# A hand-ordered attention and mixture-of-experts kernel: the written order of all engines replaced by another, and the first zero matmuls cut into more pieces

## The chip, the cores and the metric

The kernel runs on one core of a Trainium2 chip. A core has five engines with a queue of instructions each: TensorE (PE; its weight loads are shown as PEld), VectorE (DVE), ScalarE (ACT), GpSimd (POOL) and SyncE (SP), which here only issues transfers. The metric is the device time of one execution in microseconds (us); lower is better.

## The reference, cut to what matters

Two stages over 8 batches of 576 positions. The first is attention with a window of 64 keys, for 8 heads of 64; the second takes its result as input of four causal attention experts, of which each position uses two.

```python
scores = scale * np.matmul(q, k.transpose(0, 1, 3, 2))
scores = np.where((rel >= 0) & (rel < 64), scores, -1e9)
x = softmax(scores) @ v                      # heads side by side: 8 x 576 x 512
logits = x @ w_gate                          # the two largest of four, softmax over the two
for e in range(4):
    a = softmax(causal(scale * (x @ wq[e]) @ (x @ wk[e]).T))
    out += gate[e] * (a @ (x @ wv[e]) @ wo[e])
```

## The kernel before

The work is cut into units, and a unit into steps: a generator yields after each step. The string `ORDER` names a unit at each word, and each word runs the next step of that unit. Since every step only appends instructions to the queues of the engines it uses, `ORDER` alone sets in which order the work stands on all five engines. Digits behind a colon are the PSUM banks that the step takes.

The units that matter below, with their lines in the profile:

- `f`: first constants. DVE zeroes the tile `px`, and TensorE runs matmuls of zeros on it (L214). `c` and `i` are other constants (`causal`, `m_f`, `tri`).
- `m`: scores of the first stage (L337). One word computes two groups, which are 64 matmul instructions of 96 columns on a quarter of the array's columns and half of its rows, each with its own weight load. Two such words after each other are 128 matmuls and 128 loads.
- `q`: softmax of a group (DVE L349 to L386, ACT L365, POOL L362, L384, L390). `t`: its transposes (L407). `a`: product with the values (L433).
- `w`: weights split into two half-precision parts (L266 is their TensorE step). `n`, `M`, `N`: one scale per batch (L483 and L488 on TensorE, L491 on DVE).
- `v`, `k`, `r`, `o`: projections to values, keys, queries and output, all on L585 to L587, three matmuls for each product. `x` and `y`: scores and softmax of the second stage (L701, L710; DVE L721, ACT L725). `u`: its gates and splitting (ACT L772, POOL L782 and L783). `D`: transposes of the weights by a transfer, the last three on TensorE (L800). `A`: product with the values (L832, then ACT L838 and DVE L841).
- `F`: matmuls that compute nothing that is used (L874), in `keep_busy`; the number behind the underscore says how many.
- `p`, `h`, `l`: loads of queries and keys, of values, and of weights, issued by SP.

TensorE's instructions come from DRAM through a queue of their own, which the profile calls "q8 instruction".

Of the kernel before, what the change touches and what calls it, by code (L numbers as in the profile page):

```python
# [38 lines left out]


ORDER = (
# [104 lines left out]
def window_attention_moe_attention(ctx: ExitStack, tc: tile.TileContext, qT, kT, vW,  # L146
                                   wg, wq, wk, wv, wo, out):
    nc = tc.nc
# [8 lines left out]
    def bank():  # L157
        return PS[:, banks.pop(0)]
# [46 lines left out]
    def first_constants():  # L205
# [7 lines left out]
        for _ in range(8):  # L213
            nc.tensor.matmul(bank(), lhsT=px[:, 0:128], rhs=px[:, None].to_broadcast([128, 2, 256]),  # L214
                             start=True, stop=True)
# [298 lines left out]
    M2 = {}  # L514
# [475 lines left out]
```

## Time and profile before

| what | value |
|---|---|
| three runs | 414.85, 413.15, 412.34 us; median 413.15 |
| profiled execution, its own time | 414.9 us |
| its span, first to last instruction | 413.1 us |
| TensorE busy | 384.6 us, 93% of the span |
| DVE, ACT, POOL busy | 342.1, 333.3, 301.3 us |
| mean granted TensorE clock | 0.981 |
| "q8 instruction" | 56 transfers, 0.92 MB |

The span is the time from the first instruction to the last, and 1.8 us of the execution lie outside it. Busy times overlap between engines. A granted clock of 1.00 is 2.4 GHz, 0.50 is 1.2 GHz; a value between them is a stretch with some of both. In a row of waits, "A <- B" means that A stood still until B ended; "issue" stands where an engine waited for nothing that the profile shows.

### The profile page before, as it was taken

To read this page: it belongs to the slowest core of one execution; us is meant where nothing else is said; L and a number is where in the kernel's file an instruction comes from. 1 tells how busy PE (TensorE), PEld (TensorE's weight loads), DVE (VectorE), ACT (ScalarE), POOL (GpSimd) and SP (SyncE) were. 2 spreads that over 40 slices of the span, in tenths; PEclk is the share of its full clock that TensorE was granted. 3 is DMA by queue.
4 is the path that set the end of the run, shared out by engine and by line. 5 is a ranking of instruction groups with operands and counts; after the bars stand their busy time and mean duration, and the time that the engine had idled before them with its cause. 6 is when DMAs were issued, how large, how long until landed. Compare 5 with 4: busy or idle time off the path is not lost. (4 is left out here: it accounts for less than half of the span.)

```text
span 413.1 us, 18175 instructions
## 1 busy us (share of the span) xinstructions
PE 384.6 (93%) x7234; PEld 285.7 (69%) x7234; DVE 342.1 (83%) x1044; ACT 333.3 (81%) x1150; POOL 301.3 (73%) x678
## 2 busy tenths in 40 slices
PE   6879997899899998999999999999999999999884
PEld 3757874778577874777677776678677876876553
DVE  2969999987898876888999988798898898699841
ACT  1949599986999975898898899877899789879851
POOL 7346757989889986788878988688888976976300
PEclk9989999999999998999999999999999999999968
DMA  7951621699979977785984999896889852799973
GB/s 238 376 172 66 209 81 69 136 200 163 219 240 176 206 137 171 180 230 89 146 260 108 222 177 254 256 168 130 151 189 219 131 85 85 126 201 187 187 124 111
DMA packets 141732, 71.04 MB, mean 172 GB/s; under 512 B 122576, under 2 KB 125648, under 8 KB 141648
## 3 DMA queue, kind: packets, MB, share of 16 engines
q1 hardware_dynamic: 141280, 69.50, 78.2%
q8 instruction: 56, 0.92, 0.9%
q10 hardware_dynamic: 368, 0.39, 0.3%
q14 instruction: 28, 0.23, 0.2%
HBM read 30.94 MB, written 9.44 MB: 98 GB/s over the span
## 5 line engine op out<-in xcount | busy, mean ns | idle before, releaser
L783 POOL TENSOR_TENSOR sp<-p,sp 128x320 f16<-128x320 f32 (+3 forms) x110 | 100.0, 909 | 9.2
L725 ACT ACTIVATE p<-p,r 128x576 f32<-128x576 f32 (+3 forms) x128 | 77.4, 609 | 6.5 <-DVE r L721 6.4
L772 ACT ACTIVATE sp<-p,r 128x576 f16<-128x576 f32 (+3 forms) x122 | 72.7, 620 | 2.2 <-DVE r L761 0.9
L365 ACT ACTIVATE p<-ps,st 128x64 f32<-128x64 f32 x204 | 61.3, 315 | 11.6 <-POOL st L362 11.3
L721 DVE CUSTOM_DVE_ANT_0 p<-ps,causal,sc 128x320 f32<-128x320 f32 (+2 forms) x128 | 64.2, 546 | 6.2 <-PE ps L710 5.2
L782 POOL TENSOR_SCALAR p<-p,r 128x320 f32<-128x320 f32 (+3 forms) x110 | 65.4, 594 | 4.5 <-ACT sp L772 3.5
L390 POOL TENSOR_TENSOR p<-p,st 128x256 f32<-128x256 f32 x72 | 43.5, 614 | 12.7 <-DVE st L386 10.4
L411 DVE TENSOR_TENSOR pt<-ps,tri 128x1024 f32<-128x1024 f32 (+1 forms) x40 | 44.0, 1104 | 1.9 <-PE ps L407 1.9
L433 PE MATMUL ps<-pt,vt 64*64 64x128 f32 (+1 forms) x1440 | 39.2, 249 | 4.7 <-DVE r L721 1.7
L365 ACT ACTIVATION_READ_ACCUMULATOR p<-ps,st 128x1 f32 x204 | 42.5, 208 | 0.0
L710 PE MATMUL ps<-kt,qt 64*128 64x320 f16 (+3 forms) x480 | 40.4, 292 | 1.6 <-DVE pt L411 0.9
L433 PEld LDWEIGHTS ps<-pt,vt 64*64 64x64 f32 x1440 | 34.3, 133 | 11.1 <-DVE r L721 3.4
L337 PE MATMUL ps<-k,q 64*32 64x96 f32 (+2 forms) x2304 | 36.6, 245 | 5.4 <-issue 4.4
L832 PE MATMUL ps<-tu,v 128*64 128x64 f16 (+2 forms) x1056 | 39.6, 231 | 0.9 <-DMA tu<-sp 0.9
L832 PEld LDWEIGHTS <-v 128*64 128x64 f16 x1056 | 36.0, 113 | 5.5 <-issue 3.3
L337 PEld LDWEIGHTS ps<-k,q 64*32 64x32 f32 x2304 | 29.5, 106 | 12.1 <-issue 7.3
L585 PE MATMUL ps<-wvhi,xh 128*128 128x260 f16 x128 | 35.8, 279 | 1.8 <-DVE xl L460 1.4
L585 PE MATMUL ps<-xh,wqhi 128*128 128x320 f16 (+1 forms) x128 | 36.8, 287 | 0.4 <-DVE p L372 0.3
L585 PE MATMUL ps<-xh,wkhi 128*128 128x256 f16 (+1 forms) x128 | 36.7, 286 | 0.3 <-DVE v L611 0.3
L586 PE MATMUL ps<-xl,wkhi 128*128 128x256 f16 (+1 forms) x128 | 36.6, 286 | 0.0
L587 PE MATMUL ps<-xh,wklo 128*128 128x256 f16 (+1 forms) x128 | 36.6, 286 | 0.0
L587 PE MATMUL ps<-xh,wqlo 128*128 128x320 f16 (+1 forms) x128 | 36.6, 286 | 0.0
(165 smaller groups left out, 1016.0 us busy)
## 6 DMA issues: line engine op xcount, KB each, us to landing
vt<-in_vW_dram SPq DMA_DIRECT2D x16, 576.0 KB, 6.1
q<-in_qT_dram SPq DMA_DIRECT2D x14, 576.0 KB, 5.3
k<-in_kT_dram SPq DMA_DIRECT2D x14, 576.0 KB, 6.4
out_dram<-out SPq DMA_DIRECT2D x30, 256.0 KB, 2.9
tu<-sp SPq DMA_TRANSPOSE x93, 4.1
out_dram<-out SPq DMA_DIRECT2D x9, 128.0 KB, 3.0
q<-in_qT_dram SPq DMA_DIRECT2D x2, 320.0 KB, 8.3
k<-in_kT_dram SPq DMA_DIRECT2D x2, 320.0 KB, 7.7
```

What stands on the lines that cost most here:

```text
L337: nc.tensor.matmul(S1[g][o:o + 32, i, c:c + n], lhsT=q_t[r, i % 2, q0:q0 + 32], rhs=k_t[r, i % 2, k0:k0 + n], start=True, stop=True)
L365: nc.scalar.activation(pt[:, i], ps[:, i, 64:128], AF.Exp, bias=st[:, 0, z + i:z + i + 1], scale=0.125, accum_out=st[:, 1, z + i:z + i + 1])
L411: nc.vector.tensor_tensor(t, src, tri[:, None].to_broadcast([128, 2 * n, 2, 64]), op=OP.mult)
L433: nc.tensor.matmul(to, lhsT=values[d][r, h, b + e - (w == 0)], rhs=rhs, start=(e, h) not in started, stop=s == n - 1, skip_group_check=True)
L585: nc.tensor.matmul(ps, lhsT=ah, rhs=bh, start=first, stop=False)
L587: nc.tensor.matmul(ps, lhsT=al, rhs=bh, start=False, stop=last)
L721: nc.vector.tensor_tensor_reduce(out=dst, in0=src, in1=mask, scale=SC[b][:, 3:4], scalar=above, op0=OP.add, op1=OP.min, accum_out=to)
L725: nc.scalar.activation(p, p, AF.Exp, bias=r2[:, 0, x:x + 1], scale=-1.0, accum_out=r2[:, 1, x:x + 1])
L772: nc.scalar.activation(hi, p, AF.Copy, scale=by)
L782: nc.gpsimd.tensor_scalar(p, p, by, 1.0, op0=OP.mult, op1=OP.mult)
L783: nc.gpsimd.tensor_tensor(lo, p, hi, op=OP.subtract)
L832: nc.tensor.matmul(to, lhsT=V2[b % 2][:, c, a, 2 * pr + h], rhs=rhs, start=n == 0, stop=n == len(work_list) - 1, skip_group_check=True)
```

## The change

The string `ORDER` is replaced as a whole. All units and all steps are the same, each as often as before; their order and their banks differ. The `F` words differ too: five with 31 matmuls before, ten with 38 now, and the first three of them use `px` in place of `ident`. The eight matmuls of zeros of 512 columns in `f` become 53 of 73 to 86 columns, with the same columns in sum: a bank takes seven or six of them, by the digits of `FILL`.

```diff
+FILL = "77777666"
 
 ORDER = (
-    'p0 i c p1 h0 l0 f:01234567 l2 h1 p0 z p1 l1 m0:6 l3 d q0 h2 q0 e1 m1:7 q0 e0 q0 m2:5 q1 q0 m3:0 q1 n0 q1 q1 q1 '
...
+    'f:01234567 p0 c p1 l0 l2 h0 h1 z i p0 Fa0_3:0 m2:7 p1 m0:6 d l1 l3 q0 e0 q2 Fa1_4:5 m3:5 q0 q0 q0 m1:4 e1 w0 q1 '
...
 )
@@ first_constants
-        for _ in range(8):
-            nc.tensor.matmul(bank(), lhsT=px[:, 0:128], rhs=px[:, None].to_broadcast([128, 2, 256]),
-                             start=True, stop=True)
+        for n in map(int, FILL):
+            ps = bank()
+            for i in range(n):
+                c = slice(512 * i // n, 512 * (i + 1) // n)
+                nc.tensor.matmul(ps[:, c], lhsT=px[:, 0:128], rhs=px[:, 0:c.stop - c.start], start=True, stop=True)
```

The lines of the changed program are higher by four: L337 is L341 there, and so on. Three places show what the new order does. The first is the start of DVE's queue, before the first scores. Before:

```order
L225 MEMSET tri 128x128
L551 MEMSET m_f 128x128
L558 TENSOR_SCALAR causal<-m_f 64x64
L559 TENSOR_SCALAR causal<-m_f 64x64
L560 TENSOR_SCALAR m_f<-m_f 128x64
L206 MEMSET px_72 128x128
L207 MEMSET half_87 128x2
L208 MEMSET win 128x64
```

The same place on DVE in the changed program:

```order
L208 MEMSET px_72 128x128
L209 MEMSET half_87 128x2
L210 MEMSET win 128x64
L555 MEMSET m_f 128x128
L562 TENSOR_SCALAR causal<-m_f 64x64
L563 TENSOR_SCALAR causal<-m_f 64x64
L564 TENSOR_SCALAR m_f<-m_f 128x64
L229 MEMSET tri 128x128
```

Zeroing `px`, on which TensorE's first matmuls wait, moved ahead of all other constants.

The second place is on TensorE, between a product `a` of the fourth batch and the output projection of an earlier one. Before:

```order
L433 MATMUL ps<-pt_30_2836,vt_84 64x64 x4
L433 MATMUL ps<-pt_30_2836,vt_84 64x128 x12
L433 MATMUL ps<-pt_30_2836,vt_84 64x64 x4
L337 MATMUL ps<-k_2498,q_2497 32x96 x32
L407 MATMUL ps<-ident,p_33_2859 128x64 x4
L407 MATMUL ps<-ident,p_34_2902 128x64 x4
```

On TensorE in the changed program, the same product and what stands behind it; a row of L341 or L437 is two matmuls and two loads for each of its count, one of L411 is one of each:

```order
L437 MATMUL ps<-pt_30_2971,vt_84 64x64 x4
L437 MATMUL ps<-pt_30_2971,vt_84 64x128 x12
L437 MATMUL ps<-pt_30_2971,vt_84 64x64 x4
L411 MATMUL ps<-ident,p_33_2969 128x64 x4
L411 MATMUL ps<-ident,p_34_3006 128x64 x4
L589 LDWEIGHTS y_109
L589 MATMUL ps<-wohi,y_109 128x512
```

On TensorE in the changed program, a little further on, at the end of the first product of the projection:

```order
L590 LDWEIGHTS y_110
L590 MATMUL ps<-wolo,y_110 128x512
L591 LDWEIGHTS y_110
L591 MATMUL ps<-wohi,y_110 128x512
L341 MATMUL ps<-k_2611,q_2610 32x96 x32
L589 LDWEIGHTS y_109
L589 MATMUL ps<-wohi,y_109 128x512
```

The word of `m` with its 64 score matmuls moved from ahead of the transposes to behind six matmuls of 512 columns.

The third place is on TensorE in the second batch of the first stage. Before:

```order
L407 MATMUL ps<-ident,p_18_1242 128x64 x4
L407 MATMUL ps<-ident,p_19_1366 128x64 x4
L337 MATMUL ps<-k_1190,q_1189 32x96 x32
L433 MATMUL ps<-pt_16_1471,vt_84 64x64 x4
L433 MATMUL ps<-pt_16_1471,vt_84 64x128 x12
L433 MATMUL ps<-pt_16_1471,vt_84 64x64 x4
L433 MATMUL ps<-pt_17_1548,vt_84 64x64 x4
```

The same units on TensorE in the changed program:

```order
L437 MATMUL ps<-pt_16_1514,vt_84 64x64 x4
L437 MATMUL ps<-pt_16_1514,vt_84 64x128 x12
L437 MATMUL ps<-pt_16_1514,vt_84 64x64 x4
L341 MATMUL ps<-k_1244,q_1243 32x96 x32
L411 MATMUL ps<-ident,p_18_1293 128x64 x4
L411 MATMUL ps<-ident,p_19_1420 128x64 x4
L437 MATMUL ps<-pt_17_1595,vt_84 64x64 x4
```

The product of group 16 moved ahead of the scores and of the transposes.

## Rows read from the trace of the kernel before

**Rows 1.** The page, busy time, share of the span and instructions of each engine.

```profile
PE 384.6 (93%) x7234; PEld 285.7 (69%) x7234; DVE 342.1 (83%) x1044; ACT 333.3 (81%) x1150; POOL 301.3 (73%) x678
```

**Rows 2.** Windows: stretch, length, busy time (instructions) by engine, TensorE clock, DMA share, GB/s.

```profile
20.00:30.00 10.00, 6.90 (x127) 5.04 (x110) 5.92 (x17) 4.74 (x19) 4.82 (x7) 0.83 0.48 152
150.00:200.00 50.00, 47.66 (x894) 34.39 (x891) 41.15 (x127) 38.04 (x133) 38.60 (x91) 0.97 0.74 160
200.00:250.00 50.00, 49.15 (x913) 35.78 (x913) 46.53 (x145) 45.44 (x165) 41.93 (x90) 1.00 0.95 190
390.00:400.00 10.00, 7.49 (x87) 5.27 (x82) 5.96 (x19) 6.38 (x14) 0.76 (x1) 0.69 0.98 165
```

**Rows 3.** Waits of TensorE: us in total, times, longest.

```profile
PE ps L337 <- issue: 4.4, 2, 2.4
...
PE ps L433 <- DVE r L721: 1.7, 2, 1.4
```

**Rows 4.** Timeline of TensorE around three stops: start, length, instructions, idle before.

```profile
18.97 1.68 PE L337 MATMUL ps<-k,q 64*32 64x96 f32 x123
23.07 0.36 PE L337 MATMUL ps<-k,q 64*32 64x96 f32 x5 [2.42 <-issue]
...
160.38 0.36 PE L337 MATMUL ps<-k,q 64*32 64x96 f32 x6 [1.96 <-issue]
...
268.43 0.27 PE L433 MATMUL ps<-pt,vt 64*64 64x64 f32 x2 [0.68 <-issue]
```

**Rows 5.** Windows from one stop to another, the third in part of the second.

```profile
23.05:160.36 137.31, 128.15 (x2678) 98.15 (x2678) 119.70 (x350) 114.73 (x433) 105.92 (x236) 0.99 0.73 166
160.36:268.42 108.06, 105.84 (x2042) 76.42 (x2042) 95.39 (x290) 92.82 (x324) 87.05 (x188) 0.98 0.88 187
255.25:268.42 13.17, 12.30 (x255) 7.99 (x256) 10.41 (x30) 12.14 (x39) 9.90 (x20) 1.00 1.00 271
```

**Rows 6.** The page, DMA queue of TensorE's instructions: packets, MB, share.

```profile
q8 instruction: 56, 0.92, 0.9%
```

**Rows 7.** DMA queues from 13.8 to 20.6 us, all that moved.

```profile
q1 hardware_dynamic: 1434, 2.55, 97.2%
q14 instruction: 1, 0.01, 0.4%
```

**Rows 8.** DMA queues from 157 to 158 us.

```profile
q8 instruction: 1, 0.02, 5.8%
```

**Rows 9.** Windows of short stretches without a stop.

```profile
305.89:309.27 3.38, 3.38 (x127) 2.65 (x130) 3.38 (x10) 2.86 (x6) 3.13 (x7) 1.00 1.15 104
115.10:118.35 3.25, 3.25 (x138) 3.02 (x131) 3.16 (x8) 3.25 (x9) 2.09 (x6) 1.00 0.63 190
```

**Rows 10.** Windows in which the clock was at half.

```profile
25.10:28.50 3.40, 2.75 (x13) 1.92 (x13) 2.66 (x5) 3.12 (x17) 0.97 (x3) 0.50 0.84 271
161.64:165.05 3.41, 3.41 (x10) 1.18 (x8) 3.10 (x7) 0.00 (x0) 1.44 (x4) 0.50 1.02 75
393.75:400.57 6.82, 6.35 (x57) 4.19 (x56) 3.35 (x9) 2.78 (x7) 0.00 (x0) 0.50 0.83 125
```

**Rows 11.** Waits of the other engines from 155 to 170 us.

```profile
ACT out L861 <- PE ps L587: 4.4, 1, 4.4
...
DVE ps L352 <- PE ps L337: 2.6, 1, 2.6
```

**Rows 12.** Timeline of TensorE, groups of small matmuls.

```profile
154.94 1.53 PE L832 MATMUL ps<-tu,v 128*64 128x256 f16 x36
156.40 1.12 PE L433 MATMUL ps<-pt,vt 64*64 64x64 f32 x40
157.47 0.95 PE L337 MATMUL ps<-k,q 64*32 64x96 f32 x58
```

**Rows 13.** Timeline of TensorE, matmuls that keep it busy, and transposes at half clock.

```profile
3.98 3.59 PE L214 MATMUL ps<-px 128*128 128x512 f16 x8 [3.98 <-DVE half L207]
...
9.78 2.72 PE L874 MATMUL ps<-ident 128*128 128x128 f32 x22
...
394.04 1.78 PE L800 MATMUL ps<-ident_h,sp 128*128 128x128 f16 x15 [0.21 <-ACT sp L772]
```

199 rows, old and new, of the table ORDER are left out of this document.

## The prediction

> **What bounds the kernel now.** I read the busy times first. TensorE is busy for 384.6 us of 413.1, the others for 301 to 342 [rows 1], so where TensorE stands still is the first question. Windows by stage answer it: from 200 to 250 us it is busy for 49.15 of 50 us at full clock, but it loses 3.1 us of the ten from 20 to 30, 2.3 us from 150 to 200, and 2.5 us of the ten from 390 to 400, and in the same three windows the mean clock is 0.83, 0.97 and 0.69 [rows 2]. The list of waits then shows that the largest item is none of an engine's: "issue", 4.4 us in two pieces ahead of the score matmuls [rows 3]. The timeline puts them at 20.65 to 23.07 and at 158.42 to 160.38, each in the midst of an unbroken run of equal matmuls, with a third one of 0.68 us at 268.43 [rows 4]. Nothing in the program waits there: 123 matmuls of a word go through, and the last five wait for 2.42 us.
>
> What they have in common is their place in TensorE's own stream. Between the first and the second stop it ran 2678 matmuls and 2678 weight loads, 5356, which is 20 short of 21 times 256; between the second and the third 4084, 12 short of 16 times 256; and the stretch from 255.25 to 268.42 has 511, one short of two times 256 [rows 5]. The instructions that are missing are those that only wait, which the view doesn't count. The queue that brings TensorE's instructions made 56 transfers of 0.92 MB, 16 KB each [rows 6], and 14468 matmuls and loads divided by 56 are 258. So the stops are ends of a block of 256 instructions whose successor had not arrived. The Trainium skill, "Runtime: NRT & Kernel Launch", section "Instruction fetch mechanics", gives the same block (16 KiB, 256 instructions) and says that the next one is fetched while the current one executes, so that crossing a boundary is "mostly hidden". The trace agrees with the size [rows 5, 6] and disagrees with the second at these three ends, with 2.42, 1.96 and 0.68 us [rows 4]; by that rule the change would be worth nothing, which is a rival below.
>
> Why these ends and not the other fifty: from 13.8 to 20.6 us not one block came, while loads held 97.2% of the DMA engines [rows 7]; the block before the second stop came between 157 and 158 us [rows 8], and TensorE went on at 160.38. So from its start a block needs 2.4 to 3.4 us until it can be used, and its start is late where loads fill the queues. A block of instructions that TensorE finishes faster than that makes it stand. Stretches of about 256 that took 3.38 and 3.25 us show no stop [rows 9], so the limit without loads in the way is below 3.3 us.
>
> **The change part by part.**
>
> *The blocks.* I cut TensorE's order of both programs into blocks of 256 and priced their small matmuls by the timeline: a score matmul with its load 0.016 us (58 in 0.95; 0.014 in the long run of 123), a product of the first stage 0.028 (40 in 1.12), one of the second stage 0.0425 (36 in 1.53) [rows 4, 12]. Before, the block that ends at the first stop holds 124 score matmuls, 1.7 us of work; the one that ends at the second 59 scores, 40 and 29 products, 3.3 us; the one at the third 86 and 30 products and 12 wide matmuls, over 3.7 us, which was late for loads alone. In the changed order the poorest block is the third place shown: 64 scores and 52 products, 2.5 us, with eight transposes and three wide matmuls on top. The next hold 32 and 36 products with 45 scores (3.2 us and 15 others), and 34 scores with 84 products (3.0 us and ten others). The burst of 128 scores near 20 us is still there, but the pieces of `f` and the added `F` words push the block's end into its middle: 69 scores end a block that begins some 30 matmuls and 12 busy-keeping ones earlier. At the second place six wide matmuls now stand between the products and the scores. So the first stop, 2.42 us, and the second, 1.96, should go; the third, 0.68, too if the loads stand as before, since its block is mixed otherwise.
>
> What is late next there: nothing with a claim on the same time. In the second stop DVE waited 2.6 us for those scores, and ACT 4.4 us for the projection behind them [rows 11]; in the window of the first DVE is busy for 5.92 of 10 us and ACT for 4.74 [rows 2]. All engines come forward with TensorE.
>
> *The clock.* Behind the first two stops the granted clock falls to 0.50, 1.2 GHz, from 25.10 to 28.50 and from 161.64 to 165.05 [rows 10]; before that TensorE had stood for 2.42 and 1.96 us. At full clock the busy time in them is half: 2.75/2 is 1.4 us and 3.41/2 is 1.7 us less. I take 3.1; bounds 0 (the clock falls for another reason) and 3.4.
>
> *New stops.* The poorest block costs nothing if its successor starts at once (limit below 3.3 us), and up to 3.4 less 2.5, 0.9 us, if not; late by a load as in rows 7, some 2.4 us, and then the clock's 1.7 too. I take 0.5 for it and 0.5 each for the next two, in sum 1.5; bounds 0 and 6.
>
> *Zero matmuls.* They start when DVE has zeroed `px`, at 3.98 us before, and that memset is now DVE's first [rows 13]. The eight took 3.59 us. 53 pieces of the same columns take as long if the columns bound them. If a load of 128 columns bounds each, the nearest row is the transposes of 128 columns at half clock, 1.78 us for 15, 0.12 each, and 53 are 6.3 us. Either ends at 4.5 to 7.5 us after a start near 1 us, and the scores began at 7.5. I take 0, as weights and values that are still loading bound that stage; bounds -1 and 0.
>
> *More `F` matmuls.* One costs 2.72/22, 0.12 us for each of two records, so seven more cost 1.7 us [rows 13]. Most stand in the first 30 us, where TensorE waits; two words with five matmuls stand later, 1.2 us. I take 0.3; bounds 0 and 1.2.
>
> *All else* of the order: no term can be read off a table of words; bounds -2 and +3, taken as 0. The last 20 us keep their shape (transposes by TensorE between waits for splits, half clock for 6.82 us [rows 10]), with one output projection put behind the last product.
>
> The sum: -2.42 - 1.96 - 0.68 - 3.1 + 1.5 + 0.3 is -6.4 us. From the profiled execution's 414.9 this makes 408.5. Its time is 1.75 above the median of the three, 413.15, so the forecast is 406.8 us.
>
> **The rivals.**
>
> *The stops move.* Lateness follows the loads, and the new order has its own coincidences: loads of queries, keys and values stand next to the blocks with 45 and 34 scores. Two stops of 2.2 us, each with 1.6 us of clock, are 7.6 instead of 1.5; 406.8 + 6.1 is 412.9, no change. For it: the third stop befell a block that wasn't short. Against: two of the three went with the two poorest blocks.
>
> *The stops aren't the instructions.* Then another order has them somewhere else or they cost nothing once others bound the stage: 413.2 give or take 1. Rows 5 speak against it. This is what the skill's "mostly hidden" would give.
>
> *Slower.* The order pays for its long blocks with overlap: score words that stand behind six wide matmuls reach DVE later, and TensorE then waits for probabilities at L433 as it does once now, for 1.4 us [rows 3]. It decides once this happens oftener than (6.4 + 4.1)/1.4, about eight times, once in each batch: 417.3 us and more. Against it: from 200 to 250 us DVE and ACT still have 3.5 and 4.6 us of 50 free [rows 2].
>
> *The change doesn't do what it says.* A block as short as 1.7 us is gone by count, so this is only open for the poorest one, and is in its term.
>
> **How the numbers follow.** A measurement of this kernel tells about 1% from no change, 4.1 us. The forecast, with both long stops gone and the rest within its bounds, 402 to 409 us: 0.62. Stops that move, 409 to 413.5: 0.22; of it 0.02 is still faster. Not the instructions: 0.06. Slower within 1%: 0.02. Slower by more: 0.08. So faster 0.64, same 0.28, slower 0.08. The low end of the range is 406.8 less the 1.5 of new stops, 1 of the start and 2 of the rest, about 402; the high end is the second case's, 413.5. Outside lie the slower cases, 0.10, half of the 0.06, and some 0.05 of the forecast's own below 402.
>
> **What would show it.** Right: no wait of the kind "issue" over 1 us in a run of equal matmuls, a clock of 1.00 from 10 to 390 us, the matmuls of the first batch's scale (L492 there) without a stop ahead of them, and no half clock near 160 us. Wrong: a stop of 2 us at another multiple of 256, most likely in a block with 45 or 34 scores; or none, with TensorE's waits for DVE and ACT between 50 and 350 us grown by more than 4 us.

## The result, and the profile after

| | before | changed |
|---|---|---|
| median, runs beside each other (6 and 6) | 412.59 us | 408.58 us |
| again, beside the experiments (14 and 6) | 412.57 us | 408.38 us |
| profiled execution, and its span | 414.9, 413.1 us | 407.6, 405.9 us |

The ratio is 0.989, 95% interval 0.986 to 0.992, and 0.988 (0.984 to 0.992) in the second comparison: the change makes the kernel faster, by 4.0 and 4.2 us. Medians here and below are of the runs that are within 1.5% of the fastest of the same kernel. The two profiled executions lie further apart than that, 7.2 us of span, since that of before was the slowest of its first three runs and that of the changed kernel the fastest of its six. The programs of the experiments are longer or shorter by a few lines too, so that L337 of before is L338 in one and L341 in another.

The page of the changed kernel, its busy times and the queue of TensorE's instructions [rows 1, 6]:

```profile
PE 384.2 (95%) x7293; PEld 288.3 (71%) x7293; DVE 347.7 (86%) x1044; ACT 333.3 (82%) x1150; POOL 302.1 (74%) x678
...
q8 instruction: 57, 0.93, 1.0%
```

TensorE is as long busy as before, in a span that is 7 us shorter. That is not the same work at the same speed: 12.5 us of the busy time of before lie in windows at half clock [rows 10], and this profile of the changed kernel has none; its `F` words, on the other hand, are busy for 11.7 us where they were for 8.0. The same stages as in rows 2:

```profile
20.00:30.00 10.00, 9.24 (x197) 7.14 (x197) 8.96 (x24) 6.81 (x25) 6.69 (x12) 1.00 0.61 217
150.00:200.00 50.00, 48.48 (x894) 34.42 (x895) 44.23 (x137) 41.39 (x142) 42.05 (x95) 1.00 0.91 206
200.00:250.00 50.00, 49.76 (x1069) 37.97 (x1060) 44.65 (x143) 46.30 (x168) 42.16 (x96) 1.00 0.86 170
390.00:400.00 10.00, 9.45 (x128) 6.93 (x126) 4.92 (x14) 5.79 (x14) 0.00 (x0) 1.00 0.55 158
```

The stage of the first stop gained 2.3 us of work in ten, and the clock is 1.00 in all four. The head of the list of waits of TensorE [rows 3]:

```profile
PE ps L437 <- DVE r L725: 2.1, 2, 1.5
PE ps L836 <- DMA tu<-sp: 1.9, 1, 1.9
PE ps L487 <- DVE st L390: 1.4, 1, 1.4
...
PE ps L590 <- DVE xl L464: 1.0, 1, 1.0
...
PE ps L589 <- DVE v L615: 0.8, 1, 0.8
PE ps L705 <- DVE kt L680: 0.8, 1, 0.8
```

"issue", 4.4 us before, is no longer among the large items; waits for other engines and for a transfer stand there, among them two that rows 3 did not have at this size (L487 in the start, L836 in the tail). The timeline of the changed kernel at the place of the second stop, and at the only end of a block that still shows one [rows 4]:

```profile
159.89 1.12 PE L341 MATMUL ps<-k,q 64*32 64x96 f32 x64
160.95 1.01 PE L437 MATMUL ps<-pt,vt 64*64 64x64 f32 x40
...
259.40 0.57 PE L836 MATMUL ps<-tu,v 128*64 128x64 f16 x17 [0.27 <-issue]
```

The 64 score matmuls run through, and the only stop left is 0.27 us by this view.

### The profile page after: what moved, and what is told of

Same layout as the page of the kernel before. It is cut to its first block, busy times and chain, and to the rows that moved or that the text cites. A ratio compares the mean times of both kernels' runs of the same rounds, so it can differ in the third digit from the quotient of the medians.

```text
span 405.9 us, 18314 instructions
## 1 busy us (share of the span) xinstructions
PE 384.2 (95%) x7293; PEld 288.3 (71%) x7293; DVE 347.7 (86%) x1044; ACT 333.3 (82%) x1150; POOL 302.1 (74%) x678
## 4 chain that ended last, share of the span: by engine, by line
PE 63%; DVE 18%; ACT 7%; POOL 5%; issue 4%; DMA 0%; ACTq 0%; POOLq 0%; DVEq 0%
PE ps L589 13%; PE ps L590 12%; PE ps L591 12%; PE ps L714 7%; PE ps L836 6%; PE ps L341 5%; PE ps L437 5%; DVE p L725 4%; PE ps L411 2%; DVE pt L415 2%; ACT p L369 2%; DVE sp L780 2%; ACT p L729 1%; DVE ps L356 1%; ACT xh L462 1%
## 5 line engine op out<-in xcount | busy, mean ns | idle before, releaser
L776 ACT ACTIVATE sp<-p,r 128x448 f16<-128x448 f32 (+3 forms) x122 | 73.3, 619 | 2.4 <-DVE r L765 1.4
L437 PE MATMUL ps<-pt,vt 64*64 64x128 f32 (+1 forms) x1440 | 38.9, 249 | 3.6 <-DVE r L725 2.1
L836 PE MATMUL ps<-tu,v 128*64 128x64 f16 (+2 forms) x1056 | 39.4, 229 | 2.6 <-DMA tu<-sp 1.9
L437 PEld LDWEIGHTS ps<-pt,vt 64*64 64x64 f32 x1440 | 33.9, 133 | 10.5 <-DVE r L725 3.5
L836 PEld LDWEIGHTS <-v 128*64 128x64 f16 x1056 | 35.6, 111 | 7.9 <-issue 4.7
L341 PE MATMUL ps<-k,q 64*32 64x96 f32 (+2 forms) x2304 | 38.3, 245 | 0.3 <-DVE xl L464 0.3
L590 PE MATMUL ps<-xl,wqhi 128*128 128x320 f16 (+1 forms) x128 | 36.6, 286 | 1.0 <-DVE xl L464 1.0
L589 PE MATMUL ps<-xh,wqhi 128*128 128x320 f16 (+1 forms) x128 | 36.7, 287 | 0.9 <-DVE v L615 0.8
L589 PE MATMUL ps<-xh,wkhi 128*128 128x320 f16 (+1 forms) x128 | 36.7, 287 | 0.0
L591 PE MATMUL ps<-xh,wklo 128*128 128x320 f16 (+1 forms) x128 | 36.6, 286 | 0.0
L590 PE MATMUL ps<-xl,wkhi 128*128 128x320 f16 (+1 forms) x128 | 36.6, 286 | 0.0
L341 PEld LDWEIGHTS ps<-k,q 64*32 64x32 f32 x2304 | 30.1, 106 | 7.8 <-issue 2.7
```

The lines of the kernel that those rows point to most:

```text
L341: nc.tensor.matmul(S1[g][o:o + 32, i, c:c + n], lhsT=q_t[r, i % 2, q0:q0 + 32], rhs=k_t[r, i % 2, k0:k0 + n], start=True, stop=True)
L437: nc.tensor.matmul(to, lhsT=values[d][r, h, b + e - (w == 0)], rhs=rhs, start=(e, h) not in started, stop=s == n - 1, skip_group_check=True)
L589: nc.tensor.matmul(ps, lhsT=ah, rhs=bh, start=first, stop=False)
L590: nc.tensor.matmul(ps, lhsT=ah, rhs=bl, start=False, stop=False)
L591: nc.tensor.matmul(ps, lhsT=al, rhs=bh, start=False, stop=last)
L776: nc.scalar.activation(hi, p, AF.Copy, scale=by)
```

## The experiments

The theory: TensorE stops where a block of 256 instructions ends and the next one is not there yet, because loads hold the DMA engines when it is fetched; the change gains by where its blocks end. The rival: the stops belong to the work at their place, and the new order gains by overlap.

**The same order, with 90 instructions more ahead of it.** In the kernel before, only the zero matmuls are cut, into 53 pieces.

```diff
+FILL = "77777666"
...
-        for _ in range(8):
-            nc.tensor.matmul(bank(), lhsT=px[:, 0:128], rhs=px[:, None].to_broadcast([128, 2, 256]),
-                             start=True, stop=True)
+        for n in map(int, FILL):
+            ps = bank()
+            for i in range(n):
+                c = slice(512 * i // n, 512 * (i + 1) // n)
+                nc.tensor.matmul(ps[:, c], lhsT=px[:, 0:128], rhs=px[:, 0:c.stop - c.start], start=True, stop=True)
```

> The kernel before with only the zero matmuls in 53 pieces, so 45 matmuls and 45 weight loads more at the head of TensorE's stream and the same order behind them. If a stop is the end of a block of 256 instructions, every block end lies 90 instructions earlier in the program: the stop in the second group's scores at 20.65 us and the one at 158.42 us leave their places, the second vanishes or shrinks below 0.5 us (its block then ends in other work), and new ones of 2 to 3.5 us stand near 48 us and near 310 us, where blocks end in runs of small matmuls beside loads; time 411 to 417 us, no gain. If the stops belong to the work (a wait that the profile doesn't show), they stay at the same matmuls, 20.7 and 158.4 us, and the time is 412.6 us, or up to 1 us less by the pieces.

418.96 us, ratio 1.014 (1.009 to 1.019): slower than before, by 6.1 us, and more than expected. The timeline of TensorE at the two places named, in the order of time:

```profile
47.32 0.40 PE L589 MATMUL ps<-wvhi,xh 128*128 128x260 f16 x1 [2.76 <-issue]
...
308.80 1.78 PE L341 MATMUL ps<-k,q 64*32 64x96 f32 x126
313.23 0.47 PE L341 MATMUL ps<-k,q 64*32 64x96 f32 x2 [2.65 <-issue]
```

Between them, by a window of this kernel:

```profile
47.20:310.30 263.10, 252.96 (x4974) 188.97 (x4977) 228.55 (x703) 223.80 (x789) 211.21 (x465) 0.99 0.81 174
```

These are 9951 matmuls and loads, 33 short of 39 times 256. The trace also records the instructions that only wait, which no view here counts. With them, the three stretches of rows 5 hold 5376, 4096 and 512 instructions, and the one from 47.2 us to the end of the stop at 313.23 holds 9984: exactly 21, 16, 2 and 39 times 256.

In its list of waits "issue" stands eight times, 9.3 us in sum, where that of before has 5.1 in three [rows 3, 4]. The stops at 20.65 and 158.42 us are gone, others have come, and the work at all these places is what it was. So the stops do not belong to the work, and that part of the rival falls.

**The changed order with the eight wide zero matmuls**, 90 instructions fewer ahead of it.

```diff
-        for n in map(int, FILL):
...
+        for _ in range(8):
+            nc.tensor.matmul(bank(), lhsT=px[:, 0:128], rhs=px[:, None].to_broadcast([128, 2, 256]),
+                             start=True, stop=True)
```

> The changed kernel with the eight wide zero matmuls of before in place of the pieces: the new order with 90 instructions fewer at its head. Blocks: stops come back at other places, about 2 us near 249 us and 1 to 2 us near 21 us, some with 1.6 us of half clock behind them; 411 to 414 us, so the pieces are worth 2 to 5 us, by their number. If the order itself is what gains and the pieces only fill the start, 408.6 give or take 1 us and no stop over 0.5 us.

415.30 us, ratio 1.007 (1.003 to 1.011): the whole gain is gone, and 2.4 us more. Its timeline has the stop named at 249 us, later by the time lost ahead of it (the same product starts at 249.4 us in the changed kernel), and others, the longest of 1.76 us at 23.15 and 0.99 us at 163.56:

```profile
255.19 0.66 PE L435 MATMUL ps<-pt,vt 64*64 64x64 f32 x17
257.91 0.34 PE L435 MATMUL ps<-pt,vt 64*64 64x128 f32 x4 [2.06 <-issue]
```

**The changed order with 41 pieces**, 24 instructions fewer ahead of it.

```diff
-FILL = "77777666"
+FILL = "55555556"
```

> The changed kernel with 41 pieces for 53, so every block end lies 24 instructions later in its order. If the gain hangs on where the blocks end, and not on short blocks being gone from the order for good, some ends come back: stops of 0.5 to 1.5 us near 33, 48, 115 or 248 us, 1.5 to 4 us in sum, 410 to 412 us. If the order is good at any cut except the worst, 408.6 give or take 1 us.

413.18 us, ratio 1.000 (0.996 to 1.004): 24 of 14,586 matmuls and loads cost all that the change had brought, so the new order with another cut gains nothing. The profiled execution took 410.9 us and has two stops, the other of 0.91 us at 251.5. The timeline shows the first in the midst of an output projection, in wide matmuls:

```profile
157.27 0.38 PE L590 MATMUL ps<-wolo,y 128*128 128x512 f16 x1
158.96 0.39 PE L591 MATMUL ps<-wohi,y 128*128 128x512 f16 x1 [1.31 <-issue]
```

That block was not short. The window of its 256 instructions and a few more, and then the DMA queues from 150 to 156.6 us and from 156.6 to 157.6:

```profile
149.85:157.30 7.45, 7.34 (x138) 4.85 (x130) 6.56 (x24) 5.82 (x22) 6.00 (x23) 1.00 1.04 280
```

```profile
q1 hardware_dynamic: 2662, 1.77, 104.0%
...
q1 hardware_dynamic: 189, 0.34, 91.1%
q8 instruction: 1, 0.02, 6.0%
```

TensorE had 7.3 us of work in it, and yet the next block came too late, since none was fetched for 6.6 us, in which loads, output and transposes took all of the DMA engines. So the length of a block alone does not decide; when its successor is fetched does.

**One load later, TensorE's stream untouched.** In the kernel before, `p9` goes behind `m37`.

```diff
-    q32 p9 q35
+    q32 q35
...
-    m37:43 q35
+    m37:43 p9 q35
```

> The kernel before with one word moved: the load p9 (two transfers of 576 KB, issued at 152 us) 45 words later, behind m37. TensorE's stream is the same, word for word. If the block's transfer was late because loads and stores filled the queues from 153 to 158 us, it now comes 1 to 2 us earlier, the stop at 158.4 us (1.96) is below 0.6 us, the half clock at 161.6 us (1.7) is gone, and the time is 2 to 3.5 us less, 409 to 411 us; the first and third stop stay. If a block end stops TensorE by the shortness of the block alone, the stop stays at 1.5 to 2 us and the time at 412.6; if the pair's data then come too late, TensorE waits for them near 170 us.

409.86 us, ratio 0.993 (0.989 to 0.997), 3.0 us less. The timeline of its scores there, and the window of the stage:

```profile
159.05 1.00 PE L338 MATMUL ps<-k,q 64*32 64x96 f32 x64
159.98 0.27 PE L408 MATMUL ps<-ident,p 64*128 64x64 f32 x2
```

```profile
150.00:200.00 50.00, 49.65 (x992) 1.00 0.77 172
```

All 64 scores in one run: the second stop and the half clock behind it [rows 4, 10] are gone with one word for SP. By the packets in the trace, the transfer of that block now starts 0.4 us after TensorE's first instruction of the block ahead of it, where it started after 2.7 us.

**Control: the same word in the changed kernel.**

> Control: the changed kernel with its load p9 45 words later, as in e3_p9_late. It has no stop there (0.18 us at 160.6). If e3_p9_late gained by its stop alone, nothing changes here: 408.6 give or take 1.2 us. If a later load gains by itself (other transfers come sooner), 1 us or more less here too; if the pair then comes too late, TensorE waits near 170 us.

408.41 us, ratio 0.991 (0.987 to 0.994): no change against the 408.4 to 408.6 us of the changed kernel. The later load gains nothing where there is no stop.

**The old order, 56 instructions fewer**: two groups of busy-keeping matmuls are fewer and wider, the others as they were.

```diff
-    w2 Fb0_11:1 w0:7
+    w2 Fw0_3:1 w0:7
...
-    q3 Fb1_9:6 a1:56
+    q3 Fw1_3:6 a1:56
...
-    def keep_busy(n, of):
-        ps = bank()[:, :128]
+    def keep_busy(n, of, wide=False):
+        ps = bank() if wide else bank()[:, :128]
...
-            nc.tensor.matmul(ps, lhsT=of, rhs=of, start=True, stop=True)
+            nc.tensor.matmul(ps, lhsT=of, rhs=of[:, None].to_broadcast([128, 4, 128]) if wide else of,
+                             start=True, stop=True)
```

> The kernel before with its first two groups of busy-keeping matmuls (20 of 128 columns) as 6 of 512 columns: nearly the same time on TensorE, 56 instructions fewer, the order otherwise the same. Blocks: every block end lies 56 instructions later in the program; the first stop shrinks to about 1.3 us, those at 158.4 and 268.4 us go, one of 1 to 2 us comes near 118 us; 2 to 4 us less than before, 408.5 to 410.5 us, so part of the change's gain without its order. If the order is what gains: 412.6 give or take 1 us, stops where they were.

410.52 us, ratio 0.996 (0.992 to 1.000), 2.3 us less. The stops at 158.4 and 268.4 us are gone, the first is 1.00 us, and one near 118 us has come. The timeline at the first and the new one:

```profile
23.05 0.52 PE L337 MATMUL ps<-k,q 64*32 64x96 f32 x11 [1.00 <-issue]
...
116.28 1.04 PE L337 MATMUL ps<-k,q 64*32 64x96 f32 x61
119.54 0.49 PE L337 MATMUL ps<-k,q 64*32 64x96 f32 x29 [2.22 <-issue]
```

Two that were not expected stand at 172.7 and 307.9 us, of 1.19 and 0.81 us. So "issue" adds up to 5.2 us here, as much as in the kernel before (5.1), and what differs between the two profiles is the clock: 0.995 in the mean against 0.981. This run alone does not show that fewer stops made it faster.

**The same with one load later.** In the last kernel the DMA queues brought no block from 114.6 to 117.2 us (the first row is all that moved) but one from 117.2 to 118.2 (the second):

```profile
q1 hardware_dynamic: 393, 0.61, 76.6%
...
q8 instruction: 1, 0.02, 5.9%
```

```diff
-    t26 h7 u101
+    t26 u101
...
-    n3 q28
+    n3 h7 q28
```

> The kernel with 56 instructions fewer (e4_fewer), and besides the load h7 (issued at 113.5 us) 35 words later. In e4_fewer a stop of 2.46 us stood at 117.08 us; the block's transfer began at 117.30, when that load's packets had passed. Blocks, late by loads: it now begins at 115 to 116 us, the stop shrinks to 0.6 us or less, and the time is 408 to 409 us, that of the changed kernel, with the old order. If the stop stays at 2 us or more, loads aren't what makes the block late there; 410.6 us.

409.41 us, ratio 0.993 (0.990 to 0.996). The block now comes between 114.8 and 115.8 us (the queues in that stretch), and in the timeline 0.62 us are left of the stop:

```profile
q8 instruction: 1, 0.02, 8.1%
```

```profile
118.12 0.68 PE L338 MATMUL ps<-k,q 64*32 64x96 f32 x35 [0.62 <-issue]
```

The old order with two small moves is within 1.0 us of the changed kernel, which the intervals (0.990 to 0.996, and 0.986 to 0.992) can't tell apart.

**The start: `f` first in the kernel before.**

```diff
-    'p0 i c p1 h0 l0 f:01234567 l2 h1 ...
+    'f:01234567 p0 i c p1 h0 l0 l2 h1 ...
```

> The kernel before with the word f moved from the seventh place to the first: px is DVE's first memset, and the eight zero matmuls begin near 1.1 us and not at 3.98; no other word moves, TensorE's stream is the same. If weights and values that are still loading bound the first 20 us (what the prediction took, 0), the first scores start 1 to 1.4 us earlier but the stop at 20.65 us and all behind it stand where they were, give or take 0.4 us: 412.6 give or take 1 us. If the start was bound by these matmuls, all behind is 1 us or more earlier, 411.5 us or less.

412.02 us, ratio 1.000 (0.997 to 1.003). The timeline of its first matmuls:

```profile
1.12 3.25 PE L215 MATMUL ps<-px 128*128 128x512 f16 x8 [1.12 <-DVE half L208]
5.02 0.76 PE L338 MATMUL ps<-k,q 64*32 64x32 f32 x32 [0.64 <-DMA k<-in_kT_dram]
6.69 1.55 PE L338 MATMUL ps<-k,q 64*32 64x32 f32 x87 [0.91 <-DMA k<-in_kT_dram]
```

The scores start at 5.02 us, where the zero matmuls of before ended at 7.57 [rows 13], and wait for keys instead; in the time nothing is left of it. The stop at 158 us is still there and even longer, 2.83 us.

**The tail: one more transpose on TensorE** in the changed kernel.

```diff
-BY_PE = ((7, 1, 1, 1), (7, 1, 2, 0), (7, 1, 2, 1))
+BY_PE = ((7, 1, 1, 1), (7, 1, 2, 0), (7, 1, 2, 1)) + ((7, 0, 2, 1),)
...
-    u710 D7021 u710
+    u710 u710
...
-    u711 u711 D7120:1
+    u711 u711 D7021:1 D7021:6 D7021 D7021 D7120:1
```

> The changed kernel with one transpose of its tail (D of batch 7, pair 0, third part, low halves) by TensorE in place of a transfer. In the tail TensorE waits 1.9 us at 387 us for that transfer's tile; eight such transfers stand in SP's queue from 377.28 us, 1.74 us each. If the queue of these transfers bounds the tail, the wait shrinks by 1 us or more for 0.7 us of TensorE, and the last product is 0.5 to 1 us earlier: 407.5 to 408.2 us. If the tail is bound elsewhere (splits on ACT and DVE that feed the last three transposes), another wait takes its place: 408.6 us or some tenths more.

408.94 us, ratio 0.993 (0.989 to 0.997): no gain over the changed kernel. The wait for the transfer is gone from its list of waits of TensorE, which from 355 us on begins with this line:

```profile
PE ps L805 <- ACT tu L167: 2.5, 1, 2.5
```

A wait of the last transposes on TensorE for a copy by ACT took its place. So the queue of transposes alone does not bound the tail; that the chain of splits and copies does is likely from this row, but no run took that chain away.

**A second profile of the changed kernel**, for the clock.

> The changed kernel once more, for a second profile. The first had full clock throughout; most of its timed runs have a mean clock of 0.996, one half-clock stretch of 3.4 us. If the tail's full clock (390 to 400 us, 1.00; 0.69 before) is the order's, the stretch is not there but near 20 to 35 us or 60 us, where TensorE waits; if it is chance, it is at 390 to 400 us again.

408.11 us, a single run. The half clock is in windows of TensorE at and behind two waits for DVE, which begin at 61.7 and 64.7 us and last 1.5 and 1.0 us:

```profile
64.00:66.00 2.00, 1.00 (x22) 0.81 0.00 0
66.00:68.00 2.00, 2.00 (x30) 0.50 0.00 0
68.00:70.00 2.00, 2.00 (x37) 0.84 0.04 8
```

That is one of the places named, where TensorE waits. But the first profile and a third, of the run below, have the same two waits and full clock there, and the third has its half clock from 390 to 400 us:

```profile
390.00:400.00 10.00, 9.44 (x114) 0.83 0.42 119
```

The place differs from one execution to the next, with the same waits.

**Nine busy-keeping matmuls at those two waits.**

```diff
-    y001 a10:01 q16
+    y001 Fb10_6:0 a10:01 q16
...
-    g00 x011:67 a10
+    g00 Fb11_3:6 x011:67 a10
```

> The changed kernel with two busy-keeping words more, six and three matmuls of nothing ahead of the two waits for DVE at 61.4 and 64.5 us (1.85 and 1.23 us). In the second profile of the changed kernel the clock falls to 0.50 at 66 to 68 us, behind them. If the half clock comes from the engine standing there, it goes: 1.00 from 50 to 100 us, and the median is 0.5 to 1.5 us below that of the changed kernel run beside it. If the matmuls only delay what waits, or the 36 instructions bring a stop back further on, it is equal or up to 2 us slower.

> The changed kernel, timed beside e11_busy60 on the same chip, and for the size of the gain: 408.4 us, ratio 0.99 give or take 0.003.

409.45 us with them (11 runs) against 408.38 without (6), 1.1 us slower. In the timeline they stand behind the wait, not in it:

```profile
63.35 1.60 PE L879 MATMUL ps<-ident 128*128 128x128 f32 x12 [1.50 <-DVE r L726]
64.88 1.00 PE L438 MATMUL ps<-pt,vt 64*64 64x128 f32 x32
```

They themselves wait for DVE's step at L726, behind which the PSUM bank that I gave them comes free, so they delayed the products by 1.6 and 0.9 us. The clock was 1.00 from 60 to 70 us in both profiles of this comparison, so nothing follows for it.

## Why the prediction was right, step by step

**Direction and mechanism** were right: 408.4 to 408.6 us against 406.8, in the range. That the stops are ends of blocks was argued from counts [rows 5]; the shifted kernels, the exact multiples of 256 and the one moved load show it. The rule cited from the Trainium skill ("Runtime: NRT & Kernel Launch", section "Instruction fetch mechanics"), that crossing a boundary is mostly hidden, holds for most of the 56 boundaries and fails for three of them in the kernel before, for eight in its shifted one and for one in the changed kernel, by up to 2.76 us each. Of the rivals, "the stops move" describes the kernels with 41 and with eight pieces, not the changed one; "slower" falls, since the wait for probabilities is 2.1 us where it was 1.7 [rows 3].

**The size** was not: the sum is 6.4 us, the gain 4.0 to 4.2, and that it came so near is in part luck, since terms missed in both directions. The sum was also read off the slowest of three executions, with a mean clock of 0.981, and taken off their median; between the two profiled executions the span differs by 7.2 us.

**The first stop (-2.42)** went, but not all of it was gained. The prediction said that nothing was late next there; in its place TensorE waits 1.4 us for DVE at L487. DVE's first scale (L491 before, L495 now) starts at 22.2 us and not at 23.8, so 1.6 us came through. This is the step that failed at the start. The reading that no block came from 13.8 to 20.6 us made more of the loads than there is: TensorE's first instruction of the block that ran out there starts at 18.6 us, and the transfer of the next begins 2.1 us later.

**The second (-1.96)** went whole, and the moved load prices it with its half clock: 3.0 us of time for the 3.66 that rows 4 and 10 add up to.

**The third (-0.68)** went in part: the changed kernel still has one end of a block with a stop, at 259 us, of 0.27 us, and of 0.55 in the third profile. **New stops (+1.5; 0 to 6)** were none beside it. The poorest block, which the term was for, cost nothing; the kernel with 41 pieces shows that lateness by loads, up to 6.6 us, weighs more than shortness. I had priced the blocks by their work and should have priced them by the loads that stand when each is fetched, too.

**The zero matmuls (0)** are worth nothing as zero matmuls: 3.59 us for eight [rows 13], 3.63 for 53 pieces, and an earlier start alone moves nothing. In the timeline of the changed kernel:

```profile
1.12 3.63 PE L219 MATMUL ps<-px 128*128 128x73 f16 x53 [1.12 <-DVE half L209]
```

But their number is worth about 4.7 us against 41 of them and 6.8 against 8, since each adds two instructions ahead of every block's end. I saw this for the first block alone.

**The `F` matmuls (+0.3; 0 to 1.2)** are 3.7 us more of busy time. Most of them stand in the first 30 us, in which TensorE stood for 8.8 us before and for 3.7 now. What they cost in time was not measured.

**The clock (-3.1)** was of the right order, for a reason that holds only in part. Over 79 runs of the kernel before beside the experiments, the median clock is 0.988, in the 13 of the changed kernel 0.996. The eight runs of before at 0.995 and 0.996 have medians of 410.5 and 410.1 us against 412.5 for all, so some 2 us of the gain may be the clock's. It is a correlation only: these runs have no profile, and shorter stops in them would look the same. And a stop does not always bring the half clock. The windows of the stages with the stop of 2.22 us (56 fewer), of 2.06 us (eight wide) and of 2.65 us (53 pieces in the old order), one kernel each, with the clock in the third column from the right:

```profile
100.00:150.00 50.00, 46.70 (x867) 1.00 0.85 190
```

```profile
250.00:300.00 50.00, 47.74 (x937) 1.00 0.82 182
```

```profile
300.00:350.00 50.00, 46.83 (x868) 0.97 0.67 136
```

Only the last one lowered it.

**All else (0; -2 to +3)** took back some of the gain. From 350 to 380 us TensorE is busy for 1.5 us less than before, though it is not quite the same work (before, then changed):

```profile
350.00:380.00 30.00, 29.61 (x393) 1.00 0.91 167
```

```profile
350.00:380.00 30.00, 28.12 (x316) 1.00 0.92 164
```

The waits at L589 and L705 (0.8 us each) are new there, and from 300 to 350 us another 0.5 us is lost. In the tail the wait at L836 is 1.9 us and was 0.9, but the waits of the transposes for ACT have shrunk as much (two rows of before, one of the changed kernel):

```profile
PE ps L800 <- ACT sp L772: 1.4, 2, 1.2
PE ps L832 <- DMA tu<-sp: 0.9, 1, 0.9
```

```profile
PE ps L804 <- ACT out L865: 0.4, 1, 0.4
```

So the new order pays for its blocks with some 2 us of overlap behind 300 us, an estimate from these windows, inside the bounds of the term and not at its middle. No run separates it from the rest.

**The tail "keeps its shape"**: its half clock of 6.82 us [rows 10] is not there in the first two profiles of the changed kernel. But the kernel with `f` first, whose tail is that of before, also has 1.00 from 390 to 400 us. So that full clock does not need the new order.

**Open:** what decides whether a stop is followed by the half clock, why the tail's comes and goes, and how the gain divides between the stops, the clock and the overlap.

## What to carry to other kernels

Where TensorE stands in the midst of equal instructions and waits for nothing, count its instructions between two such places, those that only wait among them, and look for a multiple of 256. Then there are two cheap levers that leave the order alone: a few instructions more or fewer ahead of all (here 24 were worth about 4.7 us), or one load moved away from the moment at which the next block is fetched (3 us). An order that was searched for its blocks holds for exactly this number of instructions, and any later edit ahead of them has to be followed by a new look at all the ends.

## What was unexpected of the hardware

A block of instructions got no precedence over data: with the queues at 104% none came in 6.6 us, and a block of 7.3 us of work ran out. Over all profiles of this case there are 28 stops of 0.4 us or more. By the packets and records in the traces, each of them lies 192 or 193 instructions past a multiple of 256, and from the start of the block's transfer until TensorE goes on it takes 2.2 to 2.7 us, 2.4 in the median. In the kernel before, a transfer starts in the median about 1 us after TensorE's first instruction of the block ahead of it, and at the three stops 2.1 to 3.4 us after it. So a block of less than some 3.4 us of work, an estimate from the two medians, can be short even without loads in the way. And three profiles of one program had their half clock at 66 us, in the tail, and nowhere.
